# Six of eight weight splits finished by VectorE instead of an accumulating DMA, identity made first, and a new list of all operations

## The chip, the cores and the metric

The kernel runs on one core of one Trainium2 chip. The metric is the device time of one execution in microseconds (us). Its engines are TensorE (PE in the profile; PEld is its weight load), VectorE (DVE), ScalarE (ACT), GpSimd (POOL) and SyncE (SP); SP issues most DMAs, POOL some.

## What is computed

Three stages in a row, on 4 batches of 576 positions. First an attention with 8 heads of 64: the sum of a full attention over positions averaged in fours and a local one, where position i sees those with |i-j| < 4. Its output, 512 wide, goes through a gated layer of width 1024 and then one of width 512.

```python
out_d = sm_attn(q_d, k_d, v_d)              # q, k, v averaged in fours; 144 positions
mask = np.abs(pos[:, None] - pos[None, :]) < 4
x = np.repeat(out_d, 4, axis=2) + softmax_masked(q @ k.T / 8, mask) @ v
h = np.maximum(x @ w_in, 0.0)               # 512 -> 1024
c = conv(h, conv_w)                         # 3 taps along the sequence
x = (h * sigmoid(c)) @ w_out                # 1024 -> 512
g = sigmoid(conv5(x))                       # 5 taps, looking back
out = (g * (x @ w_val)) @ w_out2
```

q, k, v are float32. The six weight arrays come as float64 and are turned into float32 on the chip.

## The kernel before

**Precision.** The large products are made of "high" and "low" parts: a value is rounded to TensorE's fast float32 form (high) and what is left is the low part; high times high, high times low and low times high are added up in PSUM (`mm3`). Attention itself is done in plain float32.

**One list sets every engine's order.** The kernel is written as 1108 named operations. The string `ORDER` names them in one sequence; each is issued behind the last instruction of every engine before it (`in_order`), so each engine, and each DMA queue, does its share in exactly the list's order and waits at the head of its queue for what is not ready. A number behind `@` picks one of four PSUM bank pairs. Nearly all instructions carry line 172 in the profile (the helper that records them), so that one goes by tile names.

**The names.** s counts 16 pairs of heads (four for each batch), Q eight groups of two pairs, b the batch, f one of 8 slices of 128 of the wide layer, e one of 4 slices of 128 of the narrow one.
- Loads on SP: `Lk`/`Lq` (two DMAs each), `Lv0a`/`Lv0b`, `Lw0.c` (v of batch 0 for the local part: six DMAs each; `Lw0.3` is issued by POOL), `Lw`s (the same for a later pair: twelve DMAs), `Lv`s`.0`. `Lv`s`.1` to `.3` are issued by POOL and add to what `.0` brought. `Lw`s goes into one of two buffers.
- Attention: `tpk`, `tpq` (transposes on TensorE), `kT`, `qT` (ScalarE copies from PSUM), `kqd` (VectorE pooling), `sd`, `mxd`, `xd`, `smd`, `scd`, `etd`, `etc`, `avd`, `od` (pooled attention), `sl`, `mxl`, `sx`, `xl`, `sml`, `mul`, `tr`, `ava`, `avb` (local attention), `pv` (pooling of v), `xa`, `xb` (sum of both, VectorE), `xhi` (ScalarE), `xlo` (VectorE): high and low parts of x.
- Wide layer: `a`b`.`f`.`part (12 matmuls each), then `ar`, `aw` (ScalarE), `ac` (VectorE, two instructions), `at` (ScalarE), `ag` (VectorE), `ah` (ScalarE), `al` (VectorE): gate and its two parts. `b`b`.`e`.`part: 12 matmuls of the product with w_out; part p needs the gates of f = 2p and 2p+1. `y` copies it out of PSUM. `gf`, `gc`, `gt`, `yh`, `yl`, `c`, `cg`, `ch`, `cl`, `d`, `do`, `S` belong to the last layer and the output.

**The eight weight conversions** (tile `stage`, the part the change edits). Jobs 0 to 3 are quarters of w_in (tile `win`), 4 to 7 quarters of w_out (tile `wout`); each is 128 partitions by 1024 values. For job n:
- `Ls`n: SP loads 1024 KB of float64 words into one of two raw buffers, by n even or odd;
- `zs`n (ScalarE), `za`n (VectorE, two instructions), `zb`n (VectorE, two): build the float32 value in `plain(n)`;
- `zh`n (ScalarE): the high part, into win[0] or wout[0];
- `zl`n (ScalarE): minus the high part, into win[1] or wout[1];
- `Lz`n (POOL): a DMA with accumulation that adds the plain value to it, so that the low part stands there.

Job n's raw buffer is free for the next job of its parity after `zb`n. The space of wout is that of v and its local copy for batch 0, so jobs 4 to 7 write it after batch 0's attention.

**The first operations of the list before:** mask, then loads of batch 0's v, k and q, the identity matrix behind the mask on POOL, conversions 0 and 1 among the attention of batch 0, 2 and 3 behind the local v loads.

Of the kernel before, what the change touches and what calls it, by code (L numbers as in the profile page):

```python
# [53 lines left out]
etd2@3 mxd3 avb1 etc2 xa0 Lv4.1 xd3 avd2@3 mul1 tpq4@0 xb0 Lq5 tr1 tpk4@2 zs2 Lk5 smd3 ava2@1 kT4 za2
zl1 avb2@2 zb2 ava3 scd3 Lz1 avb3 Lv5.1 qT4 xhi0 kqd4 etd3@0 Ls4 etc3 xlo0 zh2 avd3 Lv4.2 sl4@0 od1 zs3
xa1 tpq5@3 xb1 zl2 tpk5@1 Lq6 za3 sd4@2 kT5 Lz2 Lk6 xhi1 a0.0.0@1 mxd4 qT5 zb3 xd4 a0.1.0@3 Lv5.2 sl5
xlo1 Ls5 zh3 a0.2.0@2 smd4 zl3 mxl2 zs4 Lz3 kqd5 sx2 a0.1.1 xl2 Lv4.3 za4 scd4 a0.0.1 sml2 ar0.1 a0.2.1  # L60
zb4 ar0.0 aw0.1 etd4@0 aw0.0 a0.3.0@3 etc4 ac0.1 Ls6 Lv5.3 zh4 a0.4.0@1 zl4 ac0.0 a0.3.1 at0.1 Lz4 mul2
at0.0 zs5 sd5@0 ag0.0 a0.4.1 ag0.1 ar0.2 mxd5 ah0.1 za5 a0.5.0@2 xd5 tr2 a0.5.1 aw0.2 smd5 zb5 scd5
avd4@0 Lv6.0 ar0.3 ac0.2 Ls7 zs6 etd5@3 etc5 za6 zh5 avd5 tpk6@3 Lv7.0 od2 al0.1 Lk7 kT6 Lv6.1 a0.6.0@0
zb6 aw0.3 zl5 tpq6@3 a0.6.1 Lq7 ah0.0 Lz5 ac0.3 qT6 zh6 Lv7.1 ava4@3 kqd6 at0.2 ava5 Lv6.2 zl6 ag0.2 xa2
ar0.4 Lz6 ah0.2 avb4@1 al0.0 at0.3 al0.2 a0.7.0@3 Lw6 aw0.4 ag0.3 zs7 ac0.4 avb5 ar0.5 a0.7.1 ah0.3 xb2
Lv7.2 at0.4 za7 xhi2 tpk7@2 Lv6.3 sl6@1 ag0.4 aw0.5 Lk8 zb7 ar0.6 Lw7 kT7 tpq7@0 ah0.4 sd6@2 qT7 mxd6
zh7 b0.0.0@0 ac0.5 xd6 sl7 Lv7.3 al0.3 xlo2 b0.0.1 Lq8 at0.5 zl7 mxl3 b0.1.0@2 aw0.6 ag0.5 Lz7 al0.4
ar0.7 sx3 ah0.5 kqd7 tpk8@3 b0.1.1 xl3 Lk9 smd6 kT8 al0.5 scd6 tpq8@1 ac0.6 b0.0.2 Lq9 qT8 sml3 aw0.7
sd7@3 etd6@1 at0.6 mxd7 b0.1.2 etc6 ac0.7 xd7 b0.3.0@1 mul3 at0.7 ag0.6 a1.7.0@3 ag0.7 ah0.6 al0.6 ah0.7
b0.3.1 al0.7 smd7 b0.0.3 tr3 scd7 kqd8 b0.1.3 y0.0 gf0.0 b0.3.2 gc0.0.0 y0.1 gf0.1 etd7@0 gc0.1.0 avd6@2  # L70
b0.3.3 Lv8.0 etc7 gc0.0.1 ava6@0 y0.3 gc0.1.1 gf0.3 avd7 Lv8.1 ava7 Lv9.0 od3 gc0.3.0 gt0.0 sl8@1 xa3
avb6@2 gc0.3.1 Lv8.2 tpk9@0 Lw8 avb7 kT9 Lv9.1 b0.2.0@0 xb3 xhi3 tpq9@2 b0.2.1 qT9 xlo3 Lv8.3 a1.7.1 Lw9
sd8@2 ar1.7 sl9 aw1.7 mxd8 kqd9 xd8 a1.4.0@3 mxl4 Lv9.2 b0.2.2 ac1.7 Lk10 Lq10 sx4 smd8 at1.7 b0.2.3 xl4
ag1.7 scd8 sml4 a1.4.1 Lv9.3 mul4 y0.2 a1.1.0@2 gf0.2 tr4 ah1.7 tpk10@1 gc0.2.0 ar1.4 tpq10@0 Lk11 aw1.4
a1.1.1 Lq11 al1.7 kT10 ac1.4 qT10 a1.0.0@3 ar1.1 aw1.1 gc0.2.1 sd9@1 at1.4 etd8@0 a1.0.1 ac1.1 etc8
gt0.1 a1.2.0@2 ag1.4 at1.1 kqd10 ar1.0 a1.3.0@0 aw1.0 mxd9 ah1.4 ac1.0 xd9 a1.2.1 al1.4 a1.5.0@3 ag1.1
at1.0 ag1.0 ah1.1 a1.6.0@1 smd9 ar1.2 al1.1 ah1.0 a1.3.1 aw1.2 al1.0 scd9 ac1.2 a1.5.1 ar1.3 a1.6.1
at1.2 aw1.3 ag1.2 etd9@2 ac1.3 ar1.6 ava8@0 ah1.2 avd8@1 aw1.6 al1.2 ava9 Lv10.0 etc9 ac1.6 at1.3 avd9
avb8@2 Lv11.0 od4 ag1.3 at1.6 tpk11@1 Lw10 xa4 Lv10.1 ar1.5 avb9 ah1.3 ag1.6 sl10@3 aw1.5 al1.3 Lv11.1
ah1.6 xb4 tpq11@0 kT11 ac1.5 sd10@2 xhi4 b1.0.0@1 qT11 xlo4 Lw11 at1.5 b1.1.0@0 mxd10 ag1.5 xd10 b1.0.1  # L80
al1.6 kqd11 b1.1.1 ah1.5 Lv10.2 smd10 al1.5 scd10 sl11 Lq12 Lv11.2 Lk12 b1.1.2 mxl5 sx5 b1.1.3 xl5 sml5
Lv10.3 etd10@2 y1.1 sd11@3 etc10 mul5 b1.0.2 Lv11.3 mxd11 tr5 xd11 b1.3.0@0 b1.0.3 smd11 scd11 avb10@2
y1.0 avd10@3 etd11@1 Lv12.0 avb11 etc11 avd11 ava10@1 Lv13.0 od5 Lv12.1 tpk12@3 Lw12 ava11 kT12 tpq12@3
xa5 Lv13.1 b1.3.1 qT12 xb5 kqd12 a2.4.0@1 xhi5 Lv12.2 xlo5 b1.3.2 Lk13 Lw13 a2.3.0@3 b1.3.3 a2.3.1
Lv13.2 y1.3 Lv12.3 sd12@2 ar2.3 Lq13 a2.5.0@0 aw2.3 mxd12 xd12 ac2.3 b1.2.0@3 a2.4.1 at2.3 smd12 scd12
ag2.3 Lv13.3 a2.5.1 ar2.4 aw2.4 a2.2.0@2 ar2.5 ac2.4 aw2.5 b1.2.1 ac2.5 at2.4 a2.2.1 ah2.3 ag2.4 at2.5
al2.3 b1.2.2 ar2.2 ag2.5 aw2.2 etd12@1 ac2.2 ah2.5 tpk13@0 etc12 tpq13@2 Lk14 ah2.4 sl12@1 al2.5 at2.2
Lq14 al2.4 ag2.2 b1.2.3 kT13 qT13 ah2.2 kqd13 sl13 y1.2 al2.2 tpk14@0 tpq14@2 Lk15 kT14 mxl6 sd13@3 qT14
Lq15 sx6 mxd13 sl14@0 xl6 kqd14 xd13 a2.1.0@2 sml6 smd13 tpk15@1 mul6 scd13 avd12@3 a2.1.1 Lv14.0 tr6
kT15 tpq15@1 ar2.1 qT15 sd14@2 Lv14.1 aw2.1 etd13@1 kqd15 sl15 etc13 mxd14 avd13 mxl7 xd14 avb12@1  # L90
Lv15.0 ac2.1 Lv14.2 sx7 avb13 xl7 smd14 ava12@2 Lv15.1 at2.1 sml7 a2.6.0@0 Lw14 scd14 ag2.1 Lv14.3 ava13
mul7 od6 ah2.1 a2.6.1 xa6 Lv15.2 xb6 etd14@3 ar2.6 tr7 sd15@2 etc14 a2.7.0@1 Lw15 mxd15 aw2.6 al2.1 xd15
a2.0.0@0 ac2.6 a2.7.1 smd15 at2.6 xhi6 ag2.6 a2.0.1 scd15 Lv15.3 xlo6 ava14@3 ah2.6 avb14@2 ar2.7 al2.6
ar2.0 avd14@1 aw2.0 etd15@0 ava15 etc15 ac2.0 aw2.7 avd15 avb15 od7 ac2.7 at2.0 a3.0.0@0 xa7 at2.7
a3.5.0@1 xb7 ag2.7 xhi7 a3.2.0@3 ag2.0 ah2.7 xlo7 ah2.0 a3.1.0@2 al2.7 END Ll4 Ll3 a3.2.1 al2.0 Ll5
a3.5.1 ar3.2 aw3.2 b2.2.0@3 ls4 ac3.2 ar3.5 ls3 a3.0.1 lw4 at3.2 aw3.5 b2.2.1 ls5 lw3 Ll0 b2.3.0@1 lw5
b2.2.2 Ll2 lh3 b2.3.1 ll3 Ll7 ac3.5 ls0 b2.2.3 ag3.2 at3.5 b2.3.2 y2.2 ag3.5 ls7 lw0 b2.1.0@3 ar3.0
aw3.0 a3.1.1 ac3.0 lh0 Ll1 b2.1.1 ar3.1 lw7 at3.0 a3.4.0@0 ll0 b2.1.2 ag3.0 ls2 lw2 a3.4.1 b2.0.0@2 lh2
Ll6 ar3.4 ll2 a3.3.0@0 ls1 ah3.0 lw1 b2.0.1 ls6 al3.0 lh1 b2.1.3 ah3.2 ll1 lw6 b2.0.2 y2.1 a3.6.0@3
ah3.5 al3.2 al3.5 aw3.1 b2.0.3 aw3.4 ac3.1 a3.3.1 y2.0 ac3.4 at3.1 a3.7.0@2 ag3.1 at3.4 ag3.4 ar3.3  # L100
a3.6.1 aw3.3 ah3.4 ac3.3 b2.3.3 ah3.1 ar3.6 al3.4 a3.7.1 at3.3 al3.1 y2.3 ag3.3 aw3.6 b3.1.0@0 yh0.1
ac3.6 b3.2.0@3 ah3.3 yl0.1 at3.6 ar3.7 b3.3.0@1 al3.3 aw3.7 ag3.6 yh1.1 b3.2.1 ac3.7 gf1.3 gf1.1 b3.1.1
gc1.3.0 yh1.0 b3.3.1 yh0.0 gc1.3.1 gf1.2 b3.1.2 at3.7 yl0.0 gf1.0 b3.2.2 ah3.6 ag3.7 gc1.0.0 ah3.7
b3.0.0@2 gc1.0.1 b3.3.2 al3.7 b3.0.1 al3.6 gc1.1.0 b3.1.3 gc1.1.1 b3.0.2 y3.1 gc1.2.0 gt1.0 b3.3.3
gc1.2.1 b3.0.3 y3.3 gt1.1 b3.2.3 y3.0 c0.3@0 lh5 yl1.1 lh6 y3.2 yl1.0 lh4 lh7 ll5 c1.0@1 ll4 ll7 cg0.3
ll6 ch0.3 c0.2@2 cg1.0 cl0.3 ch1.0 cl1.0 c0.0@3 cg0.2 ch0.2 cl0.2 c1.2@0 cg0.0 ch0.0 cl0.0 c0.1@1 cg1.2
ch1.2 cl1.2 c1.1@2 cg0.1 yh2.0 ch0.1 yl2.0 gf2.1 gf2.3 cl0.1 c1.3@3 yh2.1 cg1.1 gc2.3.0 ch1.1 gf2.0
gf2.2 yl2.1 d0@0 yh3.0 cg1.3 yh3.1 gc2.0.0 gf3.2 d1@1 gf3.3 yl3.1 gf3.0 do0 gc2.0.1 gf3.1 S0 d3@2 ch1.3
gc2.3.1 cl1.3 c2.2@3 gc3.1.0 gc3.1.1 d2@0 cl1.1 gc3.3.0 do1 do3 S1 S3 d6@1 gc3.3.1 do2 S2 gc3.2.0 d5@2
do6 yl3.0 S6 gc3.2.1 d8@0 do5 gc2.1.0 gt3.1 S5 gc3.0.0 d4@1 do8 S8 gc3.0.1 c3.1@2 gc2.2.0 gt3.0 do4  # L110
gc2.2.1 S4 c2.1@0 gc2.1.1 gt2.1 cg2.2 gt2.0 cg3.1 ch2.2 c3.2@1 cg2.1 cl2.2 ch2.1 cl2.1 d7@3 cg3.2 c2.3@2
# [925 lines left out]
```

## Time and profile before

| | us |
|---|---|
| median of three runs | 484.09 (482.45 to 488.99) |
| the profiled execution, as timed | 483.79 |
| its span, first to last instruction | 482.0 |

The page gives each engine's busy time; windows give it by stretch of the span. "PEclk" is the granted share of TensorE's clock, 1.00 for 2.4 GHz and 0.50 for 1.2 GHz. A timeline row gives start, duration, engine, operation, out<-in and, in brackets, the idle time before it and what ended it. Since each engine does its instructions in the list's order, the row of a named operation is found by counting along its engine.

### The profile page before, as it was taken

To read this page: it belongs to the slowest core of one execution; us is meant where nothing else is said; L and a number is where in the kernel's file an instruction comes from. 1 tells how busy PE (TensorE), PEld (TensorE's weight loads), DVE (VectorE), ACT (ScalarE), POOL (GpSimd) and SP (SyncE) were. 2 spreads that over 40 slices of the span, in tenths; PEclk is the share of its full clock that TensorE was granted. 3 is DMA by queue.
4 is the path that set the end of the run, shared out by engine and by line. 5 is a ranking of instruction groups with operands and counts; after the bars stand their busy time and mean duration, and the time that the engine had idled before them with its cause. 6 is when DMAs were issued, how large, how long until landed. Compare 5 with 4: busy or idle time off the path is not lost.

```text
span 482.0 us, 13345 instructions
## 1 busy us (share of the span) xinstructions
PE 439.5 (91%) x5817; PEld 405.9 (84%) x5817; DVE 326.7 (68%) x467; ACT 267.6 (56%) x516; POOL 65.6 (14%) x75
## 2 busy tenths in 40 slices
...
PEclk9755558998989899889799979999999999999999
...
GB/s 166 224 167 133 153 224 261 199 174 135 127 57 18 78 109 16 32 104 42 98 63 52 64 73 36 132 132 88 0 1 2 0 1 23 87 68 22 21 89 87
DMA packets 99300, 42.88 MB, mean 89 GB/s; under 512 B 82334, under 2 KB 93770, under 8 KB 99242
## 3 DMA queue, kind: packets, MB, share of 16 engines
...
q0 software_dynamic: 20864, 7.27, 14.0%
...
## 4 chain that ended last, share of the span: by engine, by line
PE 66%; SPq 12%; DVE 10%; DMA 7%; issue 2%; ACT 2%; ACTq 0%
PE bank L172 66%; SPq L172 12%; DVE stage L172 3%; DVE cv L172 2%; DMA ldk<-in_k_dram 2%; DMA stage<-in_moe_w_in_dram 1%; DVE late L172 1%; DMA ldw<-in_v_dram 1%; DVE w L172 1%; DMA stage<-in_moe_w_out_dram 1%; DMA stage<-in_moe_w_val_dram 1%; ACT h L172 1%; DMA ldq<-in_q_dram 1%; DVE xlo L172 1%; DVE kqd L172 1%
## 5 line engine op out<-in xcount | busy, mean ns | idle before, releaser
L172 PE MATMUL bank<-xhi,win 128*128 128x288 f32 x512 | 98.8, 305 | 0.1
L172 PE MATMUL bank<-hghi,wout 128*128 128x288 f32 x512 | 97.8, 304 | 0.4 <-ACT kq L172 0.4
L172 PEld LDWEIGHTS bank<-hghi,wout 128*128 128x128 f32 x512 | 79.2, 195 | 1.6 <-issue 0.8
L172 PEld LDWEIGHTS bank<-xhi,win 128*128 128x128 f32 x512 | 78.9, 194 | 1.7 <-issue 0.8
L172 POOL DMA_DIRECT2D vd<-in_v_dram x36 | 46.2, 1406 | 162.5 <-DMA vd<-in_v_dram 85.2
L172 DVE SCALAR_TENSOR_TENSOR cv<-h,cwt,cv 128x576 f32<-128x576 f32 x64 | 52.0, 816 | 11.2 <-ACT cv L172 10.0
L172 PE MATMUL bank<-xlo,win 128*128 128x288 f32 x256 | 56.0, 301 | 0.7 <-issue 0.7
L172 PE MATMUL bank<-hglo,wout 128*128 128x288 f32 x256 | 56.4, 303 | 0.0
L172 DVE SCALAR_TENSOR_TENSOR g<-y,cwt,g 128x576 f32<-128x576 f32 x64 | 51.3, 816 | 3.0 <-ACT g L172 1.6
L172 PE MATMUL bank<-ys,wval 128*128 128x288 f32 x384 | 51.4, 294 | 0.0
L172 PEld LDWEIGHTS bank<-ys,wval 128*128 128x128 f32 x384 | 51.1, 188 | 0.3
L172 PEld LDWEIGHTS bank<-et,ldw 32*64 32x64 f32 x1536 | 31.2, 164 | 18.4 <-ACT kq L172 6.1
L172 PE MATMUL bank<-et,ldw 32*64 32x24 f32 x1536 | 34.7, 237 | 13.1 <-ACT kq L172 5.7
L172 PE MATMUL bank<-wout,hghi 128*128 128x512 f32 x144 | 45.3, 396 | 0.0
L172 PEld LDWEIGHTS bank<-xlo,win 128*128 128x128 f32 x256 | 42.3, 194 | 0.8 <-issue 0.8
L172 PEld LDWEIGHTS bank<-hglo,wout 128*128 128x128 f32 x256 | 42.7, 196 | 0.0
L172 ACT ACTIVATE kq<-bank 128x576 f32<-128x576 f32 x32 | 20.3, 645 | 33.5 <-PE bank L172 33.4
L172 DVE TENSOR_REDUCE mxd<-bank 72x4 f32<-72x576 f32 x16 | 12.0, 749 | 31.7 <-PE bank L172 27.0
L172 PEld LDWEIGHTS bank<-wout,hghi 128*128 128x128 f32 x144 | 26.9, 188 | 6.1
L172 ACT ACTIVATE h<-bank 128x576 f32<-128x576 f32 x32 | 20.6, 647 | 20.4 <-PE bank L172 18.4
L172 ACT ACTIVATE o<-bank 128x512 f32<-128x512 f32 x18 | 10.7, 597 | 32.6 <-PE bank L172 30.5
L172 PE MATMUL bank<-wout,hglo 128*128 128x512 f32 x72 | 28.5, 396 | 0.0
...
## 6 DMA issues: line engine op xcount, KB each, us to landing
...
```

The source lines that it names most:

```text
L172: last[self.key] = getattr(self.engine, name)(*a, **kw)
```

## The change

1. For jobs 0, 1, 2, 5, 6 and 7, `zl` and `Lz` are gone. In their place VectorE subtracts the high part from the plain value in one instruction, `zt`n. Jobs 3 and 4 keep `zl` and `Lz`.
2. The list is a new one with the same other operations: 1102 names. The identity is made ahead of the mask on POOL. The load of job 0 is the first DMA on SP; the jobs are loaded in the order 0, 3, 2, 1, 4, 7, 6, 5. Jobs 0, 3, 2, 1 and 4 are converted (`zb`) ahead of batch 0's `xlo0`.
3. `load_v_first` makes its tile at the first of the two calls, whichever comes first, as `Lv0b` now comes ahead of `Lv0a`.

```diff
+LOW_BY_VECTOR = (0, 1, 2, 5, 6, 7)
 ORDER = """
-mask Lv0a Lk0 Lq0 Lv0b ident Lk1 Lq1 pv0 Lcw tpk0@0 Lk2 kT0 maskr hzero tpq0@1 Lq2 qT0 Ls0 Lw0.3 kqd0
-sl0@2 Lk3 Lq3 pv1 tpk1@3 Ls1 sd0@0 kT1 Lw0.1 tpq1@1 cws mxd0 qT1 cwv xd0 sl1 kqd1 Lw4 tpk2@3 tpq2@1 mxl0
-kT2 sd1@0 qT2 smd0 sx0 mxd1 cwt@3 scd0 sl2@1 cwc kqd2 xl0 etd0@3 zs0 sml0 sd2@2 Lw0.0 xd1 mul0 tr0 Lw0.2
...
+ident Ls0 Lcw mask Lk0 Lk1 Lq0 Lq1 zs0 Lv0b hzero maskr cws za0 Lw0.3 tpk0@0 Lq2 cwv kT0 tpk1@1 zb0
+cwt@2 tpq0@3 Lv0a qT0 tpq1@0 cwc zh0 kqd0 Ls3 sl0@2 pv1 sd0@3 kT1 zt0 Lk2 qT1 sl1 kqd1 Lk3 tpq2@1 mxd0
+Ls2 sd1@0 mxl0 xd0 pv0 sx0 xl0 Lq3 mxd1 zs3 smd0 Lw0.1 sml0 tpk2@3 scd0 za3 kT2 etd0@2 qT2 tpk3@3 zb3
+xd1 Lw0.0 sl2@1 zs2 smd1 etc0 za2 Ls1 tpq3@0 scd1 Lw0.2 avd0@2 kqd2 zh3 zb2 kT3 zl3 sd2@3 Lk4 qT3 Lz3
+Lw4 mxd2 zh2 sl3 kqd3 etd1@0 zs1 mxl1 etc1 za1 sx1 xd2 sd3@0 mul0 tpk4@3 tr0 Ls4 avd1 smd2 xl1 zb1 kT4
+ava0@1 Lq4 od0 scd2 avb0@3 Lv4.0 zt2 Lw5 zh1 etd2@2 sml1 avb1 etc2 zt1 ava1 mul1 zs4 mxd3 avd2@2 xa0 xd3
+Ls7 Lv4.1 tr1 tpq4@1 Lv5.0 za4 ava2@0 qT4 Lk5 smd3 avb2@1 xb0 scd3 Lq5 zb4 ava3 xhi0 etd3@3 xlo0 Ls6
+avb3 etc3 zs7 kqd4 Lv4.2 avd3 za7 Lv5.1 a0.0.0@3 od1 zh4 xa1 zl4 xb1 Lz4 zb7 xhi1 tpq5@2 a0.3.0@0 Lq6
...
+aw0.6 ac0.6 at0.7 avd5 tpq6@0 Lv7.0 od2 ag0.7 at0.6 Lv6.1 b0.0.0@1 Lq7 al0.2 qT6 ah0.7
+ag0.6 sl6@0 ar0.5 al0.7 Lv7.1 ah0.6 kqd6 tpk7@3 aw0.5 b0.0.1 Lk8 ar0.4 Lv6.2 ac0.5 kT7 aw0.4 b0.1.0@2
+al0.6 at0.5 Lv7.2 ac0.4 tpq7@3 b0.1.1 Lq8 qT7 ag0.5 at0.4 tr2 ah0.5 Lv6.3 sl7 ag0.4 ava4@3 Lv7.3 al0.5
+ah0.4 ava5 al0.4 mxl3 b0.0.2 zt6 sx3 xa2 b0.0.3 xl3 sml3 b0.1.2 y0.0 gf0.0 mul3 sd6@3 gc0.0.0 b0.1.3
+mxd6 b0.3.0@0 y0.1 kqd7 xd6 avb4@1 gc0.0.1 gf0.1 b0.3.1 Lw6 smd6 gc0.1.0 scd6 avb5 b0.3.2 xb2 tr3 xhi2
+b0.2.0@2 gc0.1.1 b0.3.3 Lw7 xlo2 gt0.0 b0.2.1 y0.3 gf0.3 sd7@3 gc0.3.0 etd6@1 ava6@0 etc6 mxd7 b0.2.2
...
 """
     def load_v_first(n):
-        if n == 0:
+        if "v0" not in T:
...
+    def stage_t(n):
+        hi, lo = target(n)
+        vec.tensor_tensor(
+            out=lo,
+            in0=plain(n).rearrange("p (r n) -> p r n", r=jobs[n][2]),
+            in1=hi.bitcast(F32),
+            op=ALU.subtract,
+        )
...
-        op(f"zl{n}", stage_l, n)
-        op(f"Lz{n}", stage_p, n)
+        if n in LOW_BY_VECTOR:
+            op(f"zt{n}", stage_t, n)
+        else:
+            op(f"zl{n}", stage_l, n)
+            op(f"Lz{n}", stage_p, n)
```

## Rows read from the trace of the kernel before

**Rows 1.** The page: busy time of each engine, and TensorE's granted clock in 40 slices.

```profile
PE 439.5 (91%) x5817; PEld 405.9 (84%) x5817; DVE 326.7 (68%) x467; ACT 267.6 (56%) x516; POOL 65.6 (14%) x75
PEclk9755558998989899889799979999999999999999
```

**Rows 2.** Windows: stretch, length; busy time by engine, PEclk, DMA share, GB/s.

```profile
8.00:134.00 126.00, 98.15 (x1860) 85.36 (x1861) 93.67 (x135) 81.24 (x169) 30.08 (x26) 0.76 0.94 181
...
12.00:76.00 64.00, 47.71 (x1046) 38.47 (x1045) 39.32 (x61) 33.67 (x80) 8.52 (x7) 0.55 0.88 188
...
72.00:134.00 62.00, 53.35 (x926) 49.45 (x926) 55.40 (x78) 49.82 (x93) 21.20 (x16) 0.94 1.01 181
...
96.00:108.00 12.00, 10.28 (x173) 9.09 (x172) 11.79 (x15) 11.08 (x20) 4.46 (x4) 1.00 0.80 174
...
144.00:478.00 334.00, 331.24 (x3888) 311.00 (x3887) 227.30 (x325) 178.61 (x330) 28.84 (x27) 0.96 0.25 55
```

**Rows 3.** Waits of TensorE up to 135 us: total us, times, longest.

```profile
PE bank L172 <- DVE identr L172: 10.9, 1, 10.9
...
PE bank L172 <- DMA ldq<-in_q_dram: 6.3, 2, 4.8
PE bank L172 <- DMA ldw<-in_v_dram: 4.8, 3, 2.5
```

**Rows 4.** Timeline of ScalarE, 56 to 66 us: `zs2`.

```profile
62.99 1.12 ACT L172 ACTIVATE stage<-stage 128x1024 f32<-128x1024 f32 x1 [7.77 <-DMA stage<-in_moe_w_in_dram]
```

**Rows 5.** Timeline of TensorE: from `avb2`, `avb5`, `tpk7`, `tpq8`, start of `b0.0.2`.

```profile
64.71 3.29 PE L172 MATMUL bank<-et,ldw 32*64 32x24 f32 x144 [5.55 <-ACT kq L172]
...
113.73 0.89 PE L172 MATMUL bank<-et,ldw 32*64 32x24 f32 x48
...
116.25 0.66 PE L172 MATMUL bank<-identr,ldk 96*128 96x96 f32 x6
...
133.61 0.86 PE L172 MATMUL bank<-identr,ldq 96*128 96x96 f32 x6 [4.81 <-DMA ldq<-in_q_dram]
134.18 0.83 PE L172 MATMUL bank<-hghi,wout 128*128 128x288 f32 x2
```

**Rows 6.** Timeline of SP's DMA queue: start, us to issue.

```profile
26.48 19.34 SPq L172 DMA_DIRECT2D ldw<-in_v_dram  x30
...
56.18 0.38 SPq L172 DMA_DIRECT2D stage<-in_moe_w_in_dram  x1
...
110.79 9.67 SPq L172 DMA_DIRECT2D ldw<-in_v_dram  x12
```

**Rows 7.** Tile `stage` up to 135 us: count, ns min/median/max; then its DMAs.

```profile
L172 DVE TENSOR_SCALAR stage<-stage x16: 680/694/917, 32.6 to 116.3; 128x1024 f32<-128x1024 f32 x8, 128x1024 int32<-128x1024 int32 x8
L172 DVE SCALAR_TENSOR_TENSOR stage<-stage x16: 1160/1225/1226, 34.0 to 118.8; 128x1024 int32<-128x1024 int32 x16
L172 ACT ACTIVATE stage<-stage x8: 1120/1143/1162, 26.8 to 111.3; 128x1024 f32<-128x1024 f32 x8
...
DMA to landing us min/median/max: 6.3/7.4/9.2
```

**Rows 8.** Groups by shape: busy us, mean ns of one, idle before.

```profile
L172 DVE SCALAR_TENSOR_TENSOR cv<-h,cwt,cv 128x576 f32<-128x576 f32 x64 | 52.0, 816 | 11.2 <-ACT cv L172 10.0
...
L172 DVE SCALAR_TENSOR_TENSOR cv<-cv,h 128x576 f32<-128x576 f32 x32 | 23.7, 750 | 2.6 <-ACT cv L172 2.4
...
L172 DVE TENSOR_REDUCE kqd<-kq 128x288 f32<-128x1152 f32 x16 | 21.5, 1341 | 4.1 <-PE bank L172 2.5 <-ACT kq L172 1.6
...
L172 DVE TENSOR_TENSOR xo<-bank,od 128x288 f32<-128x288 f32 x32 | 12.7, 450 | 17.6 <-PE bank L172 16.7 <-ACT od L172 0.9
...
L172 DVE TENSOR_REDUCE mxd<-bank 72x4 f32<-72x576 f32 x16 | 12.0, 749 | 31.7 <-PE bank L172 27.0 <-ACT h L172 4.3 <-ACT kq L172 0.5
...
L172 DVE TENSOR_TENSOR xlo<-xo,xhi 128x1152 fp32r<-128x1152 f32 x8 | 10.8, 1353 | 2.8 <-ACT xhi L172 2.8
...
L172 ACT ACTIVATE win<-win 128x1024 fp32r<-128x1024 f32 x4 | 4.2, 1056 | 0.0
```

More of the change, by code (lines that the diff above doesn't have):

```diff
@@ L46, in join_words @@
     )
+LOW_BY_VECTOR = (0, 1, 2, 5, 6, 7)
 ORDER = """
-mask Lv0a Lk0 Lq0 Lv0b ident Lk1 Lq1 pv0 Lcw tpk0@0 Lk2 kT0 maskr hzero tpq0@1 Lq2 qT0 Ls0 Lw0.3 kqd0
-sl0@2 Lk3 Lq3 pv1 tpk1@3 Ls1 sd0@0 kT1 Lw0.1 tpq1@1 cws mxd0 qT1 cwv xd0 sl1 kqd1 Lw4 tpk2@3 tpq2@1 mxl0
-kT2 sd1@0 qT2 smd0 sx0 mxd1 cwt@3 scd0 sl2@1 cwc kqd2 xl0 etd0@3 zs0 sml0 sd2@2 Lw0.0 xd1 mul0 tr0 Lw0.2
-etc0 tpk3@0 smd1 mxd2 scd1 tpq3@3 za0 kT3 Lk4 zb0 zs1 etd1@0 Lq4 qT3 Lw5 xd2 sl3 za1 avd0@3 mxl1 zh0
-smd2 sx1 kqd3 etc1 xl1 avd1 zb1 avb0@2 zl0 Lv4.0 Ls2 ava0@0 scd2 Lz0 Lv5.0 sd3@1 sml1 Ls3 ava1 od0 zh1
@@ L57 @@
[L57 to L111, printed above, removed]
```

53 lines of the change are left out of this document (50 added, 3 removed).

## Prediction

> **What bounds the kernel now.** I read the page first, then windows over the whole span, then TensorE's waits in the first part, then the timelines at the longest of these, and last the groups by shape for prices. The page shows TensorE busy for 439.5 of 482.0 us, with its clock at half for a stretch near the beginning and almost never later [rows 1]. The windows say where its missing 42 us are: from 144 to 478 us it is busy 331.24 of 334 us, from 12 to 76 only 47.71 of 64, and there at a granted clock of 0.55 [rows 2]. So the second two thirds are TensorE's own work, the same in both kernels, and a gain can come only from reaching that state earlier. In the first third two things hold TensorE up. Loads come late: 10.9 us for the identity, which POOL makes behind the mask, 6.3 for q and 4.8 for the local v [rows 3]. SP spends 19.34 us issuing thirty small v DMAs, and the load of conversion job 2 is issued only behind them, at 56.18 us [rows 6]. ScalarE, in the list's order, then sits 7.77 us at `zs2` with batch 0's copy `kT4` behind it [rows 4], and TensorE waits 5.55 us for that copy [rows 5]. And VectorE is full where it is not waiting: 11.79 of 12 us from 96 to 108, 55.40 of 62 (89%) from 72 to 134, against 39.32 of 64 (61%) from 12 to 76 [rows 2].
>
> **What the edit of the conversions costs by itself.** Six `zl` leave ScalarE, 6 x 1.056 = 6.3 us [rows 8]; six accumulating DMAs leave POOL and the DMA engines. Six `zt` come to VectorE. No `zt` is in the trace; the nearest row is `xlo`, the same subtraction on 1152 values, 1.353 us, so 1.353 x 1024/1152 = 1.20 us [rows 8]. The other bound is the two-input instruction on 1024 values in `zb`, 1.22 [rows 7]. I take 1.20: 7.2 us more for VectorE, five of them before the point used below. ScalarE's 6.3 us are worth nothing directly: it is busy 81.24 of 126 us there [rows 2]. A low part no longer waits for a landing (7.4 us is the median of this tile's DMAs [rows 7]), but it was always made long before its product.
>
> **What the new list moves.** It puts the load of job 0 first and jobs 3, 2, 1 ahead of most small v DMAs, and so gives VectorE conversions to do while attention's inputs arrive. By the list, job 0, 3, 2, 1 and 4 are built before `xlo0`; before, 0 to 2 were, and half of 3. The price is that k and q of pair 0 come behind 1024 KB, and that ScalarE and VectorE have `zs0`, `za0`, `zb0` at the head of their queues with `kqd0` and all of attention behind. The identity goes ahead of the mask: 10.9 us of TensorE's waiting end earlier, but the inputs then come last (job 0's load, k, q), so I count at most 2 us, and nothing for the sum, because VectorE is what paces TensorE from there on.
>
> **The sum.** I follow VectorE to `al0.4`, the last gate that `b0.0.2` needs, since from there on the new list has ready work for TensorE.
> - Start. Job 0's load is issued first, at about 0.7 us, and lands 7.4 later (the median); `zs0` takes 1.14 [rows 7]. VectorE starts in earnest at 0.7 + 7.4 + 1.1 = 9.3 us.
> - Work. Before, VectorE is busy 93.7 us from 8 to 134 us [rows 2]. Of what it did in that time the new list has these behind `al0.4`: `mxd6`, `smd6`, `kqd7`, `xa2`, `xb2`, `xlo2`, `mxl3`, `sml3`. By [rows 8] that is 0.75 + 1.34 + 4 x 0.45 + 1.35 = 5.2, and for the other three, whose rows are not shown, an estimate of 2.7 between the durations of `mxd` and `kqd`; 7.9 in all. It has these ahead that were later: `ac0.7` (2 x 0.816), `ag0.6`, `ag0.7` (0.750 each), `al0.6`, `al0.7` (taken as the same) and five `zt` (6.0): 10.6. So 93.7 - 7.9 + 10.6 = 96.4 us.
> - Fill. The new front looks to me as the stretch from 72 to 134 did: conversions mixed with attention, loads mostly ahead. I take its 89%: 96.4 / 0.894 = 107.8, and `b0.0.2` starts at 9.3 + 107.8 = 117.1 us. From 12 to 134 the list gives no place where VectorE waits long: job 3's words are due when the work ahead of `za3` ends, job 4 waits for a raw buffer that is free.
> - Against before. There `b0.0.2` starts at 134.18 [rows 5], but with six groups more behind it (`sd6`, `tpk8`, `tpq8`, `avb4`, `avb5`, `sx3`). Two local products of 0.89 and two transposes of 0.66 [rows 5] and two more of like size come to 4.3 us. The lead is 134.2 - 4.3 - 117.1 = 12.8 us.
> - Given back. In the new list the local v of pairs 6 and 7 is loaded only behind `avb4` and `avb5`, which free the two buffers. Two times twelve DMAs at 9.67 us each [rows 6] are 19.3, with a landing behind. Until `ava7` needs them TensorE has 216 matmuls; at 331.24/3888 = 85 ns each [rows 2] these are 18.4 us. So 0 to 2 us are lost; I take 1.
> - The execution profiled took 483.79 us, its span 482.0, and the median of three runs is 484.09, so its own time can stand for the median. 483.8 - 12.8 + 1 = 472.0 us.
>
> **Bounds.** What decides is VectorE's fill. At the 98% of 96 to 108 us `b0.0.2` starts at 9.3 + 98.1 = 107.4, the lead is 22.5 and the time 462. At the 74% of 8 to 134 us as a whole (93.67 of 126) it starts at 9.3 + 129.7 = 139, the lead is -9 and the time 494. I stay at 89%, nearest in the kind of work.
>
> **Rivals.**
> - *VectorE's queue stalls behind the conversions, and the kernel is slower.* `za3`, `za2` and `za1` each stand ahead of attention's `kqd2`, `mxd2`, `kqd3`, `mul0`. If the loads of jobs 3, 2 and 1 are late, each microsecond goes straight into the start of `b0.0.2`. For it: landings take up to 9.2 us [rows 7], ScalarE lost 7.77 us to just such a load [rows 4], and the DMA engines are already at 0.88 of their time from 12 to 76 [rows 2]. Against it: those loads now go ahead of most small v DMAs. It decides from a fill of 81% on: then `b0.0.2` starts at 128.9 and the lead is gone. At 78% it starts at 132.9: 483.8 - (129.9 - 132.9) + 1 = 488 us.
> - *The lead is given back later.* After 144 us the old list leaves TensorE 2.8 us of waits in 334 [rows 2]. A new list has its own: more waits for local v, or for VectorE, whose work after `al0.4` starts with the last layer's taps. If such waits cost two thirds of the lead, 8 us, the time is 480.
> - *The clock stays at half longer.* Rows: granted 0.55 from 12 to 76 though TensorE was busy three quarters of it, and 0.94 from 72 to 134; it was at full from 96 to 108 with 1.72 us of waits [rows 2]. Since VectorE paces the products `a0`, TensorE will have waits among them. If 20 us of large products more run at half, they take 10 us longer, partly in those waits; at worst the time is 482. The Trainium skill says as much for a kernel of this kind ("TensorE: Matmul & The Clock Gate", "HAM oscillation — how this bites in real kernels"): a TensorE that waits for data between groups of matmuls falls back to the slow clock and begins every group with it. The trace agrees for long waits (a load of q that cost 4.81 us is followed by two matmuls that took 0.83 us [rows 5]) and not for the short ones from 96 to 108.
> - *VectorE packs better than I think.* Conversions fill every wait for attention. At 95% `b0.0.2` starts at 110.8; nothing given back: 483.8 - 19.1 = 465 us.
>
> **How the numbers follow.** Forecast 472 us: 0.50, its own range 466 to 478. Lead given back, 480: 0.20. VectorE's queue stalling, 488: 0.13. Better packing, 465: 0.12. Clock, 482: 0.05. The range goes from 462, the time at 98% fill, to 487; above it lies most of the stalling case, about 0.1. A measurement of this kernel tells about 2% from no change: below 474.4 or above 493.8. Two thirds of the forecast, all of the better case and a little of the third make 0.50 faster; the upper half of the stalling case makes 0.06 slower; 0.44 lie within.
>
> **What would show each step.** Right: VectorE busy near 89% from 9 to 117 us in the windows; first matmul at 8 to 10 us; `b0.0.2` near 117; six accumulating DMAs fewer on POOL, six `zt` of 1.2 us; TensorE busy over 98% from about 120 us; end 10 to 13 us earlier. Wrong: a wait of VectorE or ScalarE for a load of w_in of several us between 20 and 45 us (then the fill is not 89%); TensorE waiting for `ldw` at `ava6` or `ava7` by more than 2 us, or a lead at 120 us that is not there at the end.

## The result, and the profile after

The changed kernel takes 462.08 us (median of 4 runs, 460.56 to 464.23); beside them the kernel before took 483.27 (4 runs, 480.06 to 488.99). The ratio is 0.959, 95% interval 0.951 to 0.966: faster by 4.1%. (Ratios here leave disturbed runs out, so they can differ a little from the quotient of the medians.) The forecast was 472.0, range 462 to 487. The execution profiled took 464.23 us, its span 462.5.

The page of the changed kernel, its lines that answer to [rows 1]:

```profile
span 462.5 us, 13319 instructions
...
PE 426.8 (92%) x5817; PEld 394.8 (85%) x5817; DVE 335.2 (72%) x473; ACT 262.5 (57%) x510; POOL 55.9 (12%) x69
...
PEclk9856557999999999989999999999999999999999
```

The span is 19.5 us shorter, and TensorE issues the same 5817 matmuls in 12.7 us less of busy time (426.8 against 439.5). So most of the gain is not less waiting: the same matmuls took less time. The rows below show what differs, the granted clock: the first two of `b0.0.2` took 0.83 us at half clock [rows 5] and take 0.54 here.

Windows of the changed kernel, columns as in [rows 2]; the last stretch ends at 458 because the kernel does:

```profile
8.00:134.00 126.00, 102.66 (x1833) 89.78 (x1833) 104.55 (x144) 76.48 (x162) 20.53 (x20) 0.80 0.71 144
12.00:76.00 64.00, 44.16 (x938) 35.72 (x938) 47.11 (x66) 34.41 (x79) 5.70 (x5) 0.62 0.89 196
72.00:134.00 62.00, 56.32 (x888) 52.59 (x888) 56.74 (x78) 44.77 (x87) 12.76 (x12) 0.97 0.49 89
96.00:108.00 12.00, 12.00 (x106) 11.80 (x104) 11.79 (x19) 11.41 (x26) 0.00 (x0) 1.00 0.11 26
144.00:458.00 314.00, 313.64 (x3847) 295.27 (x3844) 221.09 (x316) 176.71 (x334) 28.84 (x27) 0.99 0.27 61
...
7.50:122.60 115.10, 92.92 (x1744) 80.67 (x1744) 96.17 (x132) 72.69 (x153) 20.15 (x20) 0.78 0.77 157
```

VectorE is busier in the first third (104.55 of 126 us, before 93.67). In the last two thirds TensorE was full before too (331.24 of 334), but at a granted clock of 0.96; now it is 0.99. The last row is VectorE's share of the work up to `b0.0.2`, used below.

TensorE's waits up to 135 us (total, times, longest), which answer to [rows 3], and the timeline around the start of `b0.0.2` (last row of [rows 5]: 134.18, here 122.60):

```profile
PE bank L175 <- DMA ldk<-in_k_dram: 11.0, 3, 8.1
PE bank L175 <- issue: 9.3, 3, 5.2
PE bank L175 <- DMA ldq<-in_q_dram: 5.0, 3, 3.1
```

```profile
121.08 1.59 PE L175 MATMUL bank<-et,ldw 32*64 32x24 f32 x96
122.60 0.54 PE L175 MATMUL bank<-hghi,wout 128*128 128x288 f32 x2
122.97 0.43 PE L175 MATMUL bank<-hglo,wout 128*128 128x288 f32 x2
125.06 0.69 PE L175 MATMUL bank<-hghi,wout 128*128 128x288 f32 x4 [1.66 <-issue]
```

The 10.9 us for the identity have become 8.1 for k of pair 0, which holds the first matmul. New are 9.3 us of "issue" (before 0.7): TensorE stops inside a group and the trace shows nothing that it waits for.

**Where the 19.5 us come from.** `b0.0.2` starts at 122.6, where the forecast had 117.1. By the prediction's own reckoning the lead there is 134.2 - 4.3 - 122.6 = 7.3 us. From there to the end the kernel before takes 482.0 - 134.2 = 347.8 us, and the changed one, with 4.3 us more to do, 462.5 - 122.6 = 339.9: a further 12.2 us are gained behind `b0.0.2`, where I expected to give 1 back. Windows of the kernel before, cut where the granted clock steps (all stretches at half from 134 us to the end), and last the stretch ahead of the third:

```profile
134.00:137.40 3.40, 3.40 (x18) 3.12 (x16) 0.00 (x0) 1.88 (x3) 0.00 (x0) 0.50 0.43 97
161.30:164.70 3.40, 3.40 (x19) 3.38 (x18) 1.36 (x1) 1.81 (x2) 1.55 (x3) 0.50 0.79 101
202.30:209.10 6.80, 6.80 (x165) 5.64 (x162) 5.44 (x9) 4.63 (x8) 3.55 (x4) 0.50 0.72 98
229.60:236.40 6.80, 6.80 (x110) 6.47 (x103) 2.95 (x6) 2.54 (x4) 3.94 (x4) 0.50 0.52 72
280.80:287.60 6.80, 6.80 (x72) 6.41 (x71) 3.54 (x7) 0.85 (x2) 3.38 (x3) 0.50 0.66 91
197.00:202.30 5.30, 5.30 (x185) 4.57 (x187) 4.41 (x8) 4.62 (x9) 0.49 (x1) 1.00 0.13 29
```

They are 27.2 us in sum, with TensorE busy all the time. If the same work takes half as long at full clock, they cost 13.6 (experiment 5 has rows for this price). The changed kernel has one such stretch behind `b0.0.2`, 198.2 to 201.6 us, cost 1.7. The difference is 11.9 of the 12.2 us. (TensorE's 2.4 us fewer waits behind 144 us and its new stop of 1.66 in `b0.0.2` are the small change.) What came before each? Timeline of the kernel before, ahead of the stretch at 202.3 us: `etd9`, `ava8`, `avd8`, `ava9`, `avd9`, `avb8`, `tpk11`, then `avb9`, in which the clock falls (shown: `etd9`, `ava8`, `avd8`, `avb8`, `tpk11`, `avb9`):

```profile
197.15 0.67 PE L172 MATMUL bank<-identr,ed 72*72 72x72 f32 x8
197.74 0.90 PE L172 MATMUL bank<-et,ldw 32*64 32x24 f32 x48
198.56 0.71 PE L172 MATMUL bank<-etd,vd 72*64 72x144 f32 x8
...
200.67 0.89 PE L172 MATMUL bank<-et,ldw 32*64 32x24 f32 x48
201.49 0.72 PE L172 MATMUL bank<-identr,ldk 96*128 96x96 f32 x6
202.14 1.44 PE L172 MATMUL bank<-et,ldw 32*64 32x24 f32 x48
```

`avb8` takes 0.89 us and `avb9`, the same work, 1.44. Ahead of it stand only small attention products, one behind the other, with TensorE busy 5.30 of 5.30 us. The stretch at 134 follows the 4.81 us wait for q [rows 5]. That at 230 follows a run of the same kind, again without a wait. Those at 161 and 281 follow such runs too, but in these TensorE also stopped, for 1.33 us in `tpk9` and for 1.1 us in two stops. The new list mixes the groups of these runs with the large products `b1` and `a2`. That made the theory to test: **an unbroken run of small attention products brings the half clock, although TensorE never waits.** The rival: the stretches follow loads or waits that the front of the list sets.

### The profile page after: what moved, and what is told of

It reads as the page before. It is cut to its first block, busy times and chain, and to the rows that moved or that the text cites. A ratio compares the mean times of both kernels' runs of the same rounds, so it can differ in the third digit from the quotient of the medians.

```text
span 462.5 us, 13319 instructions
## 1 busy us (share of the span) xinstructions
PE 426.8 (92%) x5817; PEld 394.8 (85%) x5817; DVE 335.2 (72%) x473; ACT 262.5 (57%) x510; POOL 55.9 (12%) x69
## 4 chain that ended last, share of the span: by engine, by line
PE 84%; DMA 6%; DVE 4%; ACT 3%; issue 2%; SPq 1%; ACTq 0%
PE bank L175 84%; DMA ldq<-in_q_dram 4%; DMA stage<-in_moe_w_in_dram 3%; DVE stage L175 1%; ACT stage L175 1%; ACT ed L175 1%; ACT kq L175 1%; DVE cv L175 1%; DVE kqd L175 1%; SPq L175 1%; DVE win L175 0%; DVE et L175 0%; DVE el L175 0%; DVE mxl L175 0%; ACT cv L175 0%
## 5 line engine op out<-in xcount | busy, mean ns | idle before, releaser
L175 PE MATMUL bank<-hghi,wout 128*128 128x288 f32 x512 | 96.5, 300 | 1.7 <-issue 1.7
L175 PEld LDWEIGHTS bank<-hghi,wout 128*128 128x128 f32 x512 | 76.8, 189 | 2.5 <-issue 2.2
L175 POOL DMA_DIRECT2D vd<-in_v_dram x36 | 43.7, 1269 | 193.6 <-PE bank L175 102.8
L175 DVE SCALAR_TENSOR_TENSOR cv<-h,cwt,cv 128x576 f32<-128x576 f32 x64 | 51.8, 817 | 14.8 <-ACT cv L175 13.6
L175 PE MATMUL bank<-hglo,wout 128*128 128x288 f32 x256 | 55.1, 296 | 0.0
L175 PEld LDWEIGHTS bank<-hglo,wout 128*128 128x128 f32 x256 | 41.2, 189 | 0.0
L175 PEld LDWEIGHTS bank<-et,ldw 32*64 32x64 f32 x1536 | 27.6, 154 | 5.1 <-issue 4.0
L175 ACT ACTIVATE ed<-bank,mxd 72x144 f32<-72x144 f32 x64 | 23.2, 371 | 15.3 <-DVE mxd L175 15.3
L175 PE MATMUL bank<-et,ldw 32*64 32x24 f32 x1536 | 30.3, 229 | 0.4 <-issue 0.4
L175 ACT ACTIVATE h<-bank 128x576 f32<-128x576 f32 x32 | 20.8, 649 | 12.5 <-PE bank L175 6.9
```

Of the source, the lines that this page charges most:

```text
L175: last[self.key] = getattr(self.engine, name)(*a, **kw)
```

## The experiments

| run | median us (lowest to highest, runs) | ratio to before, 95% |
|---|---|---|
| e1_edit | 478.47 (473.57 to 487.39, 10) | 0.991 (0.985 to 0.997) |
| e2_list | 466.25 (463.80 to 470.23, 4) | 0.966 (0.956 to 0.977) |
| e3_front | 479.81 (476.09 to 486.18, 10) | 0.994 (0.988 to 1.000) |
| e4_tail | 475.44 (474.71 to 479.38, 4) | 0.989 (0.980 to 0.998) |
| e5_spread | 485.72 (484.15 to 490.38, 4) | 1.020 (1.011 to 1.029) |
| e6_gather | 474.59 (470.42 to 477.11, 10) | 0.990 (0.985 to 0.994) |
| e7_load | 457.65 (456.35 to 460.79, 4) | 0.960 (0.951 to 0.970) |
| e8_ident | 482.38 (478.05 to 488.08, 8) | 1.010 (1.003 to 1.016) |
| e9_two | 482.09 (475.68 to 486.26, 10) | 0.988 (0.982 to 0.993) |
| e10_ls3 | 457.36 (454.55 to 460.18, 4) | 0.943 (0.933 to 0.953) |
| e11_add | 461.27 (459.36 to 465.42, 6) | 0.961 (0.954 to 0.968) |
| e12_after | 460.73 (458.51 to 462.56, 6) | 0.958 (0.952 to 0.964) |

The medians of before beside them were 483.64 (e1 to e4), 482.61 (e5 to e8), 484.42 (e9, e10) and 483.01 (e11, e12). "Half-clock time" below is read from the granted clock of the one profiled execution of each; experiment 5 shows how far it differs between executions of one list.

**1. The edit alone, and the list alone.**

```diff
 # e1_edit: ORDER of before
-... zl0 Lz0 ...
+... zt0 ...
 # e2_list: ORDER of after, LOW_BY_VECTOR = ()
-... zt0 ...
+... zl0 Lz0 ...
```

> The list of before, with the six zt in the places of the six zl and without the six Lz. Theory (the list carries the whole difference): 483 us, within 4 us of before; VectorE 7 us busier, ScalarE 6 us less, TensorE's waits up to 135 us the same within 1 us. Rival (the fewer accumulating DMAs and the lighter ScalarE carry it): 470 us or less, with most of the gain ahead of 140 us.

> The list of the changed kernel, but each zt made again by zl on ScalarE and the accumulating DMA Lz behind it. Theory (the list carries the difference): 462 to 468 us; ScalarE's 6.3 us lie in its idle time. Rival (the list works only because zt takes no DMA time while the loads saturate the DMA engines): 475 us or more, with longer landings of the w_in and w_out words before 75 us.

The list carries some 17 of the 21 us, but not all: the edit by itself gains 4 to 5 us (ratio 0.991, medians 478.47 and 483.64). In e1's trace the waits for q fall from 6.3 [rows 3] to 1.6 us and those for `ldw` from 4.8 to 2.2, and `a0.0.0` starts at 73.1 instead of 76.2. In e2's trace `b0.0.2` starts at 129.2 us. So the theory that the list carries the whole difference missed.

**2. What of the edit it is.** ScalarE's six `zl` are kept, and VectorE adds the plain value in place of the DMA:

```diff
-        in1=hi.bitcast(F32), op=ALU.subtract,
+        in1=lo.bitcast(F32), op=ALU.add,
...
-... zt0 ...
+... zl0 zt0 ...
```

> The changed kernel with the six zl made by ScalarE again, as before, and VectorE adding the plain value to them in place of the accumulating DMA: VectorE's instruction count and the DMAs are those of the changed kernel, ScalarE's work that of before. Theory (the 4 us by which e2_list is slower are DMA time: the accumulating DMAs make the loads of the conversions land later): the time of the changed kernel within 1.5 us, w_in and w_out words landing in 8 us at the median. Rival (they are ScalarE's 6.3 us): 466 us as e2_list.

> The changed kernel itself once more, on the chip of e11_add. Both theories: 460 to 464 us, one stretch at half clock or none behind 140 us.

461.27 against 460.73: ScalarE's 6.3 us are worth nothing that shows. `b0.0.2` starts at 119.7 in e11, 118.6 in e12. That leaves the accumulating DMAs themselves for e2's loss. The page has the issue-to-landing time of the w_in loads (the last number, a median in us; for w_out it gives none), for e2_list:

```profile
stage<-in_moe_w_in_dram SPq DMA_DIRECT2D x4, 1024.0 KB, 8.0
```

and for e11_add:

```profile
stage<-in_moe_w_in_dram SPq DMA_DIRECT2D x4, 1024.0 KB, 6.3
```

In the two executions of the changed kernel it is 6.9 and 7.0. So the words land 1 to 1.7 us later beside the six accumulating DMAs, as the theory says (though in 6.3 us in e11, not the 8 expected), and VectorE waits 14.4 us behind conversions in e2, 3.9 in e11 (9.5 and 7.1 in the changed kernel). That they cost some 4 us is likely and not shown: the intervals of e2 and e11 overlap, and their place in POOL's queue, ahead of its v loads, was not tested apart.

**3. One half of each list.**

```diff
 # e3_front: ORDER of after up to b0.0.2, then what is left as in before
 # e4_tail: ORDER of before up to qT8, then what is left as in after
```

> The new list up to b0.0.2, then all that is left in the order of the list of before; zt as in the changed kernel. Theory (the two halves of the list gain separately, 7 us ahead of 140 us and 12 us behind it, there by three stretches at half clock that the old tail has behind runs of small attention products): 476 us, with half-clock stretches again between 195 and 290 us. Rival (the later gain is a result of the front, which finishes conversions and loads earlier): 464 us and no half clock behind 150 us.

> The list of before up to qT8 (just behind b0.0.2), then all that is left in the order of the new list; zt as in the changed kernel. Theory (the two halves gain separately): 471 us, start of b0.0.2 at 133 to 135 us as before, and at most one stretch at half clock behind 145 us. Rival (the later gain is a result of the front): 480 us or more.

Both theories missed: by the medians the halves bring 4 and 8 us, together 12 of 21, by the ratios 3 and 5. In e3 `b0.0.2` starts at 120.2, so the front keeps its lead there; then the seam puts `sl7 ava4 ava5`, `avb4 avb5 sd6 sx3 tpk8 tpq8 sd7 etd6` nearly back to back, and the clock is at half from 122.5 to 139.5, and again at 160 (3.4 us), 201 (10.2) and 232 (3.4): 34 us behind `b0.0.2` (with waits at the seam, TensorE busy 14.14 of 17.00 us). The rival, no half clock behind 150, is out: with the new front the old tail has its stretches in the old places. In e4 they are at 136 (6.8) and 207.7 (10.2), the latter at the one place where the new tail has a run of small groups. Why the halves don't add up is in part shown (e3's seam made a run of its own) and in part open.

**4. Runs gathered in the new list.** The products that stood between the small ones go behind them:

```diff
-... avd8@2 Lq12 aw1.6 b1.3.0@3 ... avb9 ... b1.3.1 ... sd10@0 mul5 ava9 ...
+... avd8@2 Lq12 aw1.6 ... avb9 ... sd10@0 mul5 ava9 b1.3.0@3 b1.3.1 ...
...
-... etd10@0 y1.0 b1.2.1 ... b1.2.2 etd11@0 Lv12.1 b1.2.3 ... avb11 ...
+... b1.2.1 Lv11.3 etd10@0 y1.0 ... etd11@0 ... avb11 b1.2.2 b1.2.3 y1.2 ...
...
-... xl7 b2.2.0@0 ... b2.1.0@2 ... b2.2.1 ... avb12@1 b2.1.1 ... avb13 ...
+... xl7 ... avb12@1 ... avb13 b2.2.0@0 b2.1.0@2 b2.2.1 b2.1.1 ...
```

> The changed kernel, its list changed only in that the large products b1.3.0, b1.3.1, b1.2.2, b1.2.3, b2.2.0, b2.1.0, b2.2.1 and b2.1.1 stand behind the small attention products they stood between. Theory (runs of small attention products bring the half clock): half-clock time behind 140 us rises from 3.4 us to 12 us or more in two or three stretches, each at the end of such a run, near 200, 225 and 280 us, and the time to 466 to 470 us. Rival (the order of groups does not matter for the clock): 462 us within 1.5 us and no new stretch.

474.59 us, 12.5 above the changed kernel, outside of all its runs, and above the 470 expected. Windows of e6_gather, ahead of and inside the three stretches:

```profile
186.00:194.40 8.40, 7.15 (x297) 5.73 (x299) 8.22 (x11) 5.96 (x10) 2.49 (x3) 1.00 0.42 77
194.40:201.20 6.80, 6.80 (x64) 6.75 (x58) 6.69 (x13) 3.95 (x13) 4.03 (x5) 0.50 0.78 96
...
218.30:231.90 13.60, 12.48 (x187) 11.29 (x188) 0.14 (x1) 2.21 (x6) 3.55 (x3) 0.50 0.29 47
268.00:283.10 15.10, 13.27 (x403) 11.68 (x403) 12.41 (x20) 11.62 (x21) 3.37 (x3) 1.00 0.16 22
283.10:290.00 6.90, 6.90 (x97) 6.85 (x90) 6.72 (x13) 3.66 (x14) 3.87 (x5) 0.51 0.69 87
```

Three stretches where expected, 27.3 us behind 140 us where the changed kernel has 3.4 (e2 has 3.4 too; e7, e10, e11 and e12, with the same order there, have none): up to 12 us by the clock. Waits came too: from 144 to 458 us TensorE is busy 307.99 us against 313.64, so some of the 12.5 us are waits, as small groups wait for each other. In the old list the same clock came without any wait (5.30 of 5.30 us, above), so it comes without waits too.

**5. Runs broken in the old list,** first at four places, then at the two plain ones:

```diff
 # e5_spread and e9_two
-... a1.5.1 ar1.3 a1.6.1 ... avb8@2 Lv11.0 ...
+... ar1.3 a1.6.1 ... avb8@2 a1.5.1 Lv11.0 ...
-... avb11 etc11 avd11 ava10@1 ... tpq12@3 xa5 Lv13.1 b1.3.1 ... b1.3.2 ...
+... avb11 b1.3.1 etc11 avd11 ava10@1 b1.3.2 ... tpq12@3 ...
 # e5_spread alone
-... b0.3.3 Lv8.0 etc7 gc0.0.1 ava6@0 y0.3 gc0.1.1 gf0.3 avd7 Lv8.1 ava7 ...
+... Lv8.0 etc7 gc0.0.1 ava6@0 gc0.1.1 avd7 Lv8.1 ava7 b0.3.3 y0.3 gf0.3 ...
-... avd12@3 a2.1.1 ... tpq15@1 ar2.1 qT15 sd14@2 ... ava12@2 ... a2.6.0@0 ... a2.6.1 ...
+... avd12@3 ... tpq15@1 qT15 sd14@1 a2.1.1 ar2.1 ... a2.6.0@0 smd14 ava12@2 a2.6.1 ...
```

> The kernel before (zl and Lz kept), its list changed only in that large products stand between the small attention products: b0.3.3 behind ava7, a1.5.1 behind avb8, b1.3.1 behind avb11, b1.3.2 behind ava10, a2.1.1 behind sd14, a2.6.0 and a2.6.1 around ava12. Theory (an unbroken run of small attention products, with TensorE busy all the while, is followed by a stretch at half clock): half-clock time behind 140 us falls from 24 us to 10 us or less, and the time to 476 us. Rival (the half-clock stretches follow something else that the front of the old list sets, a load or a wait): the stretches stay, 483 us within 3 us.

> The kernel before (zl and Lz kept) with three large products moved in its list: a1.5.1 behind avb8, b1.3.1 behind avb11, b1.3.2 behind ava10; nothing else. Theory (breaking a run of small attention products takes away the half clock behind it, and nothing else changes): the stretches near 200 and 230 us, 6.8 us each in the trace of before, are gone or 3.4 us at most, those near 161 and 281 us stay; 4 to 7 us less than before, 477 us. Rival (a run that is broken only moves its stretch to the next run): half-clock time behind 140 us stays at 20 us or more, and the time at 483 us within 2.

Windows of e9_two over the two places where the trace of before has 6.8 us at half each:

```profile
196.00:210.00 14.00, 13.78 (x374) 12.33 (x373) 11.37 (x17) 11.45 (x20) 3.72 (x4) 1.00 0.39 56
225.00:237.00 12.00, 11.63 (x265) 10.37 (x264) 1.76 (x5) 3.85 (x9) 1.93 (x3) 1.00 0.25 41
```

In e5 too the granted clock is 1.00 in both, while the traces of before, e1, e3 and e8, where these two runs are whole, all have both stretches. So breaking a run takes its stretch away. But "nothing else changes" fell: in e9 the stretch at 281 is gone as well, that at 160 is 6.8 us instead of 3.4, and a new one of 6.8 stands at 293, behind `ava14 avb14 avd14 etd15 ava15`, a run that was there before without one. Half-clock time behind 140 us is 13.6 us against 23.8. By the ratio the time is 6 us below before, as forecast, by the medians of all runs only 2.3. In e5 the last edit made `sd14` wait 0.74 us for a copy and changed the run around `sl15`: 13.6 us at half from 270, 3.4 new at 301, and TensorE busy 289.75 of 296 us from 144 to 440 (before 293.24). Half-clock time behind 140 fell only from 23.8 to 20.4, waits came, and the forecast of 476 was wrong: 485.72 is 3 us above before, 2% by the ratio.

How far can such totals be trusted? e1 and e8 keep the list of before, entry for entry, behind `b0.0.2`. Windows from there to the end, of before, e8 and e1:

```profile
134.18:482.00 347.82, 341.21 (x3958) 320.35 (x3956) 232.99 (x332) 185.10 (x346) 28.84 (x27) 0.96 0.24 54
134.36:480.10 345.74, 338.42 (x3959) 317.24 (x3957) 232.97 (x332) 184.86 (x346) 28.82 (x27) 0.97 0.24 55
131.06:472.20 341.14, 335.14 (x3959) 314.67 (x3957) 235.51 (x337) 185.95 (x349) 28.80 (x27) 0.98 0.25 56
```

In these stretches the clock is at half for 27.2, 20.4 and 13.6 us. That gives the price: from the first to the last row, 13.6 us less at half go with 6.1 us less busy time of TensorE and 6.7 us less time. It also shows that one list has different stretches in different executions: those near 200 and 230 us are in all three, that at 281 only in before, and that at 161 is missing in e8, behind the same run with a stop of 1.16 us. So e9's missing stretch at 281, and the totals of e5 and e9, prove nothing about their edits; the two broken runs do. Which run gets a stretch, and how long, the list alone does not tell; I leave that open.

**6. The identity alone.**

```diff
-mask Lv0a Lk0 Lq0 Lv0b ident Lk1 ...
+ident mask Lv0a Lk0 Lq0 Lv0b Lk1 ...
```

> The kernel before with one entry of its list moved: ident ahead of mask. Theory (k and q of pair 0 land late anyway and VectorE paces TensorE later): first matmul at 8 to 10 us in place of 10.9, b0.0.2 less than 1 us earlier, time within 2 us of before. Rival (the early start is kept): 480 us or less with b0.0.2 2 us or more earlier.

First matmul at 8.0 us, `b0.0.2` at 134.4 (before 134.2), and no gain: the medians are alike, the ratio is even 1% above. A by-product settles the rival about the clock. Window of e8_ident:

```profile
12.00:107.00 95.00, 75.67 (x1410) 65.34 (x1393) 69.68 (x101) 61.91 (x133) 19.30 (x15) 1.00 0.93 195
```

and of the kernel before:

```profile
12.00:107.00 95.00, 77.45 (x1436) 66.37 (x1437) 69.50 (x101) 61.97 (x134) 18.21 (x14) 0.69 0.92 193
```

Full clock against 0.69, and VectorE has done the same (69.68 and 69.50 us). In the first 107 us the clock of TensorE costs nothing that shows. In the new list it is the same: e11 ran at full clock throughout and e12 at half for 47.8 us, and `b0.0.2` came at 119.7 and 118.6 us.

**7. The small v loads out of the way of w_out.** SP issues Lw4 and Lw5, twelve DMAs each, ahead of Ls4 and Ls7. The timeline of SP's queue in the changed kernel (start, us to issue; compare [rows 6]), and VectorE's longest wait from 7 to 123 us:

```profile
44.75 7.87 SPq L175 DMA_DIRECT2D ldw<-in_v_dram  x12
52.72 0.38 SPq L175 DMA_DIRECT2D stage<-in_moe_w_out_dram  x1
...
55.56 8.37 SPq L175 DMA_DIRECT2D ldw<-in_v_dram  x12
64.05 0.38 SPq L175 DMA_DIRECT2D stage<-in_moe_w_out_dram  x1
```

```profile
DVE stage L175 <- ACT stage L175: 9.5, 5, 5.8
```

```diff
-... Lz3 Lw4 mxd2 ... Lv4.0 zt2 Lw5 zh1 ... Lk6 aw0.0 ...
+... Lz3 mxd2 ... Lv4.0 zt2 zh1 ... Lk6 Lw4 Lw5 aw0.0 ...
```

> The changed kernel with Lw4 and Lw5, 24 small DMAs, moved on SP from ahead of the w_out loads Ls4 and Ls7 to behind Lk6. Theory (VectorE's fill up to b0.0.2 was 84% and not 89% because SP issued these 24 for 16 us ahead of Ls4, Ls7, Lk5 and Lq5): VectorE's 5.8 us wait at za7 and TensorE's 3.1 us wait at tpq5 go, b0.0.2 starts at 117 to 119 us, 457 to 459 us. Rival (the DMA engines are full up to 75 us, so the loads only change places; or another wait of VectorE takes the place): b0.0.2 at 121 us or later, 461 us or more.

457.65 us, the wait at `za7` gone (longest 2.3), `b0.0.2` at 118.0: each as the theory says. But e12, the changed kernel unaltered and on the same chip, had `b0.0.2` at 118.6, a wait of 3.7, and 460.73. So the same kernel's front differs by 4 us between executions, and what the move gives is at most some 3 us; the ranges overlap (456.35 to 460.79, 458.51 to 462.56). It is faster than before; that it beats the changed kernel is not shown, and the ratios to before, 0.960 and 0.958, don't say so.

**8. The stop inside `sl1`.**

```diff
 # on top of e7_load
-... Ls3 sl0@2 pv1 ... Lk3 tpq2@1 ...
+... sl0@2 pv1 ... Lk3 Ls3 tpq2@1 ...
```

> The kernel of e7_load with one more entry moved: Ls3, 1024 KB of w_in words, behind Lk3 on SP. Theory (TensorE stops in the middle of sl1 because its next instructions are themselves fetched by the DMA engines, behind the words of Ls3): the stop of 5.25 us, with no wait that the trace shows, falls to 1.5 us or less, and the instruction packet of 16 KB, at 20.7 us before, comes at 19 us or earlier; conversion 3 comes some 5 us later, so the time is 455 to 461 us. Rival (the stop belongs to sl1 itself or is set by something other than the load): it stays at 4 us or more.

The theory fell. Timeline of TensorE in e10_ls3:

```profile
17.53 1.06 PE L172 MATMUL bank<-kq 64*24 64x32 f32 x90
24.55 0.31 PE L172 MATMUL bank<-kq 64*24 64x32 f32 x6 [5.95 <-issue]
```

The stop is as long as before, and at the same matmul: in the changed kernel, e7 and e10 alike after 90 of `sl1`'s 96. The instruction packet came at 21.4 us, not earlier. The time, 457.36, is that of e7.

## Why the prediction was right, and which steps failed

Faster was forecast, and the time, 462.08, lies at the lower end of the range; the size was 10 us short. That the time lies in the range at all is in part luck: the lower end, 462, was priced by VectorE at 98% fill, and the fill was 84 to 87%; the microseconds came from TensorE's clock behind `b0.0.2`, which the range did not count.

- *Start and work of VectorE: right.* `za0` starts at 7.5 us (9.3 forecast; the first matmul at 8.1). The 7.4 us taken for the load was a median over loads and accumulating DMAs together; `zs0` starts at 6.39, 5.7 us after the load of job 0 was issued. Up to `b0.0.2` VectorE is busy 96.17 us, in e12 96.27; the working gave 96.4. A `zt` takes 1.22 us, the upper bound.
- *Fill: too high.* 96.17 us in 115.1 is 84%, in e12 96.27 in 111.1 is 87%, forecast 89%. The lost time is the sign that the prediction named: ScalarE waits for w_in words (4.2 us at `zs1`) and w_out words (9.7 us in three waits), and VectorE behind it 9.5. My line that the list gives no place where VectorE waits long missed SP: 16 us of small DMAs ahead of job 7's load. So `b0.0.2` came at 122.6 and 118.6 us, forecast 117.1, and the lead was 7.3 to 11.3 us, not 12.8.
- *The edit by itself: priced too low.* I counted the DMAs that leave as nothing. e1 (0.991, interval to 0.997) and e2 against e11 put them at some 2 to 5 us, the second with intervals that overlap; the DMA engines were at 0.88 of their time from 12 to 76 us [rows 2]. ScalarE at nothing was right in the new list (e11).
- *Given back: wrong in sign, the largest error.* Forecast -1, measured +12.2 in the profiled execution and +12.4 in e12 (482.0 - 134.2 + 4.3 against 458.3 - 118.6). Against e8's and e1's execution of the old list it would be 10.1 and 5.5, so the size hangs on the execution and the sign does not. The step that failed is the sentence that the last two thirds are "TensorE's own work, the same in both kernels", with the reading that the clock is at half "almost never later": six slices of PEclk from 132 us on are at 7 or 8 tenths [rows 1]. The row that prices it stood there too: 0.96 over 334 us [rows 2] is 0.04 x 334 = 13 us for a list without half-clock stretches. I read a busy share of 99% as a floor. The wait for `ldw` that I charged did not show: TensorE is busy 313.64 of 314 us.
- *Rivals.* Stalling conversions: the waits came, the break-even fill of 81% was not reached. Lead given back later: the opposite. Clock at half longer: the front does run at half (0.62 from 12 to 76), and e8 shows that it costs nothing there. The page of the Trainium skill that I cited for it ("TensorE: Matmul & The Clock Gate", "HAM oscillation — how this bites in real kernels") explains the slow clock by gaps between groups of matmuls. The stretch at 202 us came with TensorE busy 5.30 of 5.30 us ahead of it, so here the measurement decides against gaps as the only cause.
- *The two errors add up,* in the executions profiled: -1.5 to -5.5 us at the front and +13 behind give 8 to 12 us more than forecast; measured are 472 - 462 = 10.
